# A new order of instructions and PSUM banks, and two buffers cleared on another engine, in a Conformer layer

## The chip, the cores and the metric

The kernel runs on one core of a Trainium2 chip, in one launch. The metric is the device time of that core in microseconds, the median of several runs. PE is TensorE, ACT is ScalarE, DVE is VectorE, POOL is GpSimd and SP is SyncE, which here only issues DMA transfers.

## The reference

Two sequences of 4000 tokens with 144 channels go through a Conformer layer in bfloat16. Each of its four parts normalises its input and adds its result to x; a last normalisation ends the layer:

```python
h = silu(layernorm(x) @ w_ff1a) @ w_ff1b;  x = x + 0.5 * h
q, k, v = split(layernorm(x) @ w_qkv)               # 4 heads of 36 channels
x = x + softmax(q @ k.T * 36 ** -0.5) @ v @ w_o     # over all 4000 keys
a, b = split(layernorm(x) @ w_pw1);  h = a * sigmoid(b)
x = x + silu(sum(pad(h)[i:i + T] * dw[i] for i in range(5))) @ w_pw2
h = silu(layernorm(x) @ w_ff2a) @ w_ff2b;  x = x + 0.5 * h
return layernorm(x)
```

## The kernel before

**Tiles and stages.** The 8000 tokens are 16 chunks of 500, eight to a sequence, and a chunk is four blocks of 125. For each chunk there is `pre` (first feed-forward part `ff1`, then `pre2` with queries, keys and values), then the attention of its 500 queries over all keys of its sequence (62 key tiles of 64 rows and one of 32 for all four heads), then `post1` (output projection, gated unit) and `post2` (convolution, second feed-forward part, last normalisation, store). The first sequence's `pre` makes the front; attention then runs from end to end of the kernel with the `pre` and `post` work of other chunks between; the rest of the last chunks' `post` makes the tail.

**One attention tile.** PE makes scores of four heads as four matmuls of 64x64 quads into two PSUM banks (`scores`). Then ACT takes the exp of both banks at once (`emit_exp`, 818 times), or, for 190 tiles, DVE does it with integer arithmetic in five instructions (`dve_tile`). PE multiplies the result by the values in four more quads (`o_quads`, called PV below), accumulating in banks 6 and 7. Banks 0 to 5 are shared by the scores and all other matmul results.

**Normalisations.** `ln` takes statistics on DVE, makes 1/sqrt with a pow on POOL (RS), and writes the normalised rows to a slot of XN, on POOL in the front's whole chunks and in the middle, on DVE for the first three chunks and in the tail. A slot has 640 columns, 576 of them used, and the rest must be zero because whole slots are transposed. So `ln` clears a slot at its first use, on POOL: 64 columns for a half chunk and all 640 for a whole one. `setup_dw` clears AN, the four slots for the attention's output, in one POOL instruction. A whole chunk is transposed in part by DVE (32x32 blocks), then by SP through DRAM (`blocks`: four transfers to `rows`, two back to XT or XTQ); `transp` clears the second half of an XT slot before its first use in this way, on POOL. Half chunks of the front and tail are transposed by PE instead.

**What sets the order.** The kernel is written as generators, and a planner (`Sched`, `pick_any`) with its own costs runs them and records every instruction with `Rec.op`, on which all instructions of a profile therefore have one line (L398). What is recorded between two steps of the planner on one engine is a block. `Rec.reorder` then moves the blocks of each engine by a table, ORDER: one character is the distance by which one block moves from its recorded place, its index in ALPHABET less 45; `~` begins a longer distance of two more characters. PLACES gives the PSUM bank of each of the 1724 results in recorded order. `reorder` derives the waits on PSUM banks from the order on PE and from PLACES; `finish` turns all dependences into semaphore waits, and `replay` writes one instruction stream for each engine. So ORDER and PLACES say what stands behind what on each engine, SP's DMA queue among them, and the planner's own times don't reach the chip.

Of the kernel before, what the change touches and what calls it, by code (L numbers as in the profile page):

```python
# [12 lines left out]
D = 144  # L13
# [5 lines left out]
LP = 80  # L19
FF = 576  # L20
KCONV = 5
TB = 125
# [17 lines left out]
        "PPPPPPQOQOPPPPPRPNPPQQQQLPPQORPNPRPTMORNNVO~OLNOMrMMNPMMNNNOMNNNOPLMQMMMNNPMMNSMNLMMOOPNSOMQMSPNOPU["  # L40
        "OMNRMOPPQIRMSNPNePNOOOcNNNNNNNNNOOLbNLOOQNSH]MMOLOMPMMOOOVPNOOOOPPPTOOOTPMUQMSLNNQQNQOQQNPPPPPTPPROK"
        "PPPPPPPPPPPP`PPPQKVPPKPPMPPRPUPPPROQQQRZOQQQRRKQRRSJPRRRRRRRWSZRNYUR~NHQ@R[KEGOOOPPPPKQOPPSPPSLPQMTP"
        "PPLQQQMPPPQVPPQOX_PTOPPCRTQQRGSQIQQSQRNV8OOQNNVSNOOLOPUUNN_MMWLNNRMMMMOOOPPPPPPQQNPPRSNRSSSORRVTR[OR"
        "AKQ@PPLOOQQNPPPPPUOOOOOPQOPPPPPUOOOOQRPLU`NNNXMMPNLQMNLZRNL`MN_YLLMK`KMNLILNQJMOOOPNYOPNOOOQNNZ^NNNN"
        "OOPNQNQOYP]CNNNNOMPMSO[NKOOQNVMPMMN`NbYMMMMNOMNIcLLNL[MMMNNQNRMJQLLROQSPLRNOQOPUQOMPQMPPRPVPLQOMQNPQ"
        "QQQSKPQSQKQQQQJPPPPPWQQSPKKQQUPPPSWPQRPQAVPPPQCVPQRPWHSYPHSOPQYPQEPQCPRZUPPSOOHDPR^OKOOOOPNOOOO^NOQN"
        "NOOOSNNNNS[NNNdRMNRKYNJWJNNNNNNGOOPP^YNNNNOMNNNNRNNPPPVROOLOOPPRZNNOOOOOPNOSOPNRPSMOOPQOQWNRPRLLNSZP"
        "NPQOIOQOTPPPRPQ]P^USPMMQIQKQQ8QTQQGMRRTQQKRRRRGLRSOMRPQQQJQQRPVP[OOOQEROO^IOQLNOOPPTTOMNQ[FOQNPPSPPM"
        "HPQOQQUPLOPNVPNOOSQNLUOOPNOXPPPLTQNLMPPPQOPPTOOPTPLOOQRNOPPPQOVPNOOOORZOP[PPMOOFRZOL[ROQKQTUBOKNFPPP"
        "_OOOOOOPNOOOOWNNVNNXMNTKMNOMZQOSLNOMSPSLLTPMOOUOPNOOTQOMOPPPQOPPPQOPPPTTQOSQSSSSNEEPQOPTPTMOMORSNNOP"  # L50
        "ROYPQOPQ^NPNPQOPAOOOOOSOOOPPPQQNPPPPPPXOOOOOOOaNPPPLOOOPUMOOOO[IOOPSOOQNPHPSWOOPPPPQGPPPPQQQMPPQQNPQ"
        "O_OOOPZOOOPI_NNNNZOPEOQWP^HKPHSJOLNOO`VPMRJOM^J`MPNKUNLUGNLJQNRIOPPRXOMOOOOPXMOPPMOOOPWOOPPPTKNOOPPP"
        "PPPPPPPQRPSYSQNQYZPRRRADIOXQGVOPJOORPIPPRRSSMR]MHOOQQQVRKNHPLPPPPPPPPPPRZQSQRRbHSGNQGPPQRRGLPQKQQQQJ"
        "QOQRPMQOPPQOSQNRMTROTNPXQQQEPJOQNPRPN_OPPPLRSOPLPPPGPPPSeOMPPQRJZPKLNNNN`NOKOVJNNNNcM`LMMMNNN]MNL]LL"
        "LLLLTWLXKMMVNQ_LMOPPQQ>MOOOTOMRbMMOOOOOTOOOQZIOPJMOOcOMPPT[PRORPEVHOPYCJQOQQGMOQQNQWNQNPPLSP_OaOOOPN"
        "PDPPPLOHPPQLPPPPQOTPNWNPPPWJNPPP`OIOPPPPPPPUQOELRP^TTQOZUPPCGOPQDJPPPPPPRPQWPRURPMFQQ_RPXDPQJLPNOJPN"
        "PPPPPSPPQ`PPTQQRERPQIQTNDPTPPJOPQQNPPUOPPSLPMPPRPQQRPJP[RNQQLaRJQSS[IQMGQQRPCZJPQOPQTPP@RPIPPPPQQQSS"
        "VXUQGNTQSSETDS`OQSCJQQdLOINQMRLLZMNSMMMMZLWPK]JMNLMTLNNNNVN`NNNNNROOPPJQOPLRPRMOQQRPLPXQQQRPTUQHFPQJ"
        "PPPPPPSPROUSPPTLPUOCOPNQOPROTWPRWRPVRZOY^YEOOPPMQ:;QDQQQQQQQQQEQQQMQOROVSMOTTQLVHROTRGNTVPHRPTRaJSQE"
        "QRSKNRNOQOPWQO=OOPNYOOOQNNOO]QOL_PNRO^NOUIPNK_MMW>MMMZMMMM]MMQLMMSNNOMOPPSOVNNPNXNPQOKQOQLQQQQUPPPHO"  # L60
        "QORPQMQOPQQSQOUVWNWMNOKOAOQOPPPPZWNNNOOLNNR^MNVNOMNNNNPSMN]NTNNNNNaNNNOQLN[RNOMRNHMSOSNPQGPQOPRXRPQW"
        "KOHOPPQYPPZPQRCO[I^NORFNNIZMMMNOWLNNNQMNRORRO_KPNOOOYNNNNNNOU^NSUHNKOJNOSOOQRJUPROTYMHNNURNNTMIPNQOU"
        "OOV[MNLNNNPYTNeJLNORNNGOO[]NNNNIQLMRLNRWOPUOO]OM`QO;LSOLO]JOJPRLLMRUNZMOVR[NPDOT^OOOFOSTOMNOSbPQLPRS"
        "_MORR_NPP^OHCNNNOZOWL~NHLMMNNNSOOXNOQQNSSOIVKPNPN]NOOOOOPPVOOOITNPPLPPQOWPPMRPNTKOOTNOPUMOOOQN`OOOPN"
        "OOPPPLOZOQQMPIQO^YROQQRLENO_PNPPPTQNNOROOSVO]QMNRNOPWTNOMNSOPQXbOOOQ[NO~NCdIMMMMMMMfbKMMMQMMJLMPLMUM"
        "MMNL^TR^JSLJQJUKPNLHQMPP`UNNNNOMOOOOPNOOPPPPQQNPQQQMUQQMSOPTQOPTPQUNQSPSQ<TRSSVEQQQHQQFPPPPPQSPMYTOL"
        "NNTMNNNP^[NOMNNQMMOLNN]PNOOR[OPKQN_ZLNESMOOKHOM[NPPLPNOOPPMQSTMNPQQQQRSQRRTCQVNGRNOMTTTMMNUPPQHNQSPM"
        "YVTQKLLSSOIJPSSPTMKORNOQOPPPPPPSORNSMRNRRRNQQRPFRPQQQQQQRPFQO"
    ),
    "act": (  # L70
        "PPPPPPPPPPPPPRSNNOSOOOPPPPPPPUPNOXNNOOOOOQNPPPPPPPPPROOPPQOPPPQOPPPPPPQQNPPPPPPPPPPPPPPPPPPPPPPPPPQO"
        "PPPPPPPPPPPPPPPPPPPPPPPPPPPPPPPPPPPPPPPPPPPPPPPPPPPPPPPPPPPPPPPPPPPPPPPPQOROSNOOPPPPPPPPPPPPPPPPPPPP"
        "PPPPPPPPPPPPPQOPPPPPPPPPPPPPPPPPPPPPPPPPQOPPQOPPPPPPPPPPPPPPPPPPPPPPPPPPPPPPPPPPPPPPPPPPPPPPPPPPPPPP"
        "PPPPPPPPPPPPPPPPPPPPPPPPPPPPPPPPPPPPPPPPPPPPPPPPPPPPPPPPPPPPPPPPPPPPPPPPPPPPPPPPPPPPPQOPPPPPPPPPPPPP"
        "PPPPPPPPPPPPPPPPPPPPPPPPPPPPPPQOPPQOPPPPPPPPPPPPPPPPPPPPPPPPPPPPPPPPPPPPPPPPPPPPROOPPQOPPPPPPPPPPPPP"
        "PPPPPPPPPPPPPPPPPPQOPPPPPPPPPPPPPPPPPPPPPPPPPQOQOPPPPPPPPPPPPPPPPPPPPPPPPPPPPPPPPPPPPPPPPPPPPPPPPPPP"
        "PPPPPPPPTOPNOPPPPPPPPPPPPPPPPPPPPPPPPPPPPPPPPPPPPPPPPPPPPPPPPPPPPPPPPPPQOPPPPQOPPPPPPPPPPPPPPPPPPPPP"
        "PPPPPPPPPPPPPPPPPPPPPPPPPPPPPPPPPPPPPPPROOPPQQNPPPPPPPPPPPPPPPPPPQOPPPPPPPQOPPPPPPPPPPPPPPPPPPPPPPPP"
        "PPPPPQOPPPPPPPPPPPPPPPPPROOPPPPPPPPPPPPPPPPPQOPPPPPPPPPPPPQOPPPPPPPPPPPPPPPPPPPPPPPPPPPPPPPPPPPPPPPP"
        "PQOPPPPPPPPPPPPQOPPPPPPPPPPPPPPPPPPPPPPPPPPPPPPPPPPPPPPPPPPPPPPPPPPPPPPPPPPQOPPPPPPPPPPPPPPPPPPPPPPP"  # L80
        "PPPPPPPPPPPPPPPPPPPPPPPPPPPPPPPPPQOSPNRNOQOUQNPMOPPPRORNQNPPPPPPQOROQQMPPPPPPQOPPPWORNNNOO"
    ),
    "dve": (
        "PPROQQQLPPPUUNNNNSMUNNPNOQOSPNSUMOPLOPTPNPNPPQQQQQQQQHPVPRPLPLPPPRSSNRNQVPUOODNUMPNPNPPQSPMXNOOQNNOO"
        "PPPPPPPSOOOPPQOPPPPPPPPPPPPPPPPQOQOPPPPPPROQQMQOQOPPQORSQMQQQQQRPQWQRPQLPQQQVQQQSUKTQ2KMPQQQRRORPQQR"
        "RRTQQRTTPP;RPQBPPSOOORPNSOPRPQKQOPPPPPPcPQcQQQQTPPERPDLDNRNRNQQQRFQNQQNQOPQOPPPQOPPPPPPPPPPPPPPPQQTM"
        "PPRPQQQQUQOQUQQQSQRVGPPPPSPPRPQQ/PQOPPSPPQQKPPPPPQOPPPPQOPPPPPROOPQQNROQNPPPPQOPQOQQNPPPQTQOPQRPSPRR"
        "NSPPRPQQQ;QOPPPPPPPPPPPROOQOPSOOOPQOROOUSUOOQSQHRGOPPPPROOPPQRPMQRNQNQOPPPPPPPPPPQOPRPRPQKQOPQQQRPQQ"
        "QQQWROOPQO?PPPPPPPPQOPSOPQePPROOPPEOPNOPNOOOOOQNPPPPPROOPPPPRPRRRRJQKPPQOPPPPPPPPPPPQOPPPYOOPNPRMSMR"
        "LQMPPQOPPPPPPPPPPPPPPPPPQOROOPROOPPPPPPPPQOPQOQOPPROOTOOOOQOSOOOPROQNPPPPPPPPPPPQSPPLQOPPPROOPPPPPPP"  # L90
        "PPPQOPPPPPPPPPPQOPPPPPQOPPPPPPPQQVPLTPMOLPPRPNPQOPPRRNNPROQNPPPPPPPPPPQOQOQORORNOPROOPPPQQNPPPPQOPQR"
        "NOPQOPPPPPSPNOQQNQOPQOPPPPPQQQMPPPPPPPQOPPPQOQRPMROQQMPPQOPSPNOPPUOOOOOWOOOOOOOPPQOPPQQQQRPRPQGPPPPP"
        "PPPPPPQOPPPPUOOOPNPQOSOOSNOSNZQMPLOPNOOOPPPPPPQQNQOQOPPPPQOQOPPPRUOUQOUIOJOOPPPQOPPPPUOOOOOPPPQOROQT"
        "QOPJQOPPPPPPPQQQMPQOPPQRNTNTNNNQNQOPQOROQNPPQOPPPPPPSPNOTOOOOPPPQOQQUPVQOTHPNIQOVOPPMPQMPTOPPRLTNOOO"
        "PPPPPPUOOOOOPQOPPSPSQSQSQUSTEOELQOPPPPPPPSOPNPPROOVOOPNOOPPROOVOOPNOOPQRPUQQQVRUQUPCKPDPPPPQOPPPPQOP"
        "QOQOSPNOhQOPPPPPHOPNOPPQOROQNGOOPPPQOQOPQOPRPNPPPPQOPPPPPROTPPLQRULVOUOJPNJPPQOQOPRPQMPPPPPPPPQQQQQK"
        "QRNRNORPNUOUP[LNKPMRNRNLNQSSMRMRPKQOQQNQOWPPMQOXOPRPNSOWNCPNORNRTTPJSQMSPPQRZOROQQQQTPUHOPRO4PPPPPPQ"
        "QQRLRPQLPPPPPPPPPQOQQQMPPPPPQQQMPPPPPPPPPQQQSLTRPSQJQQQQQRTOPPRPRSQSQRRTQUPQTDO/OPS]NSMOLNQQNLOVQUPU"
        "OKHPLRRNNPPPQOPQRPQQQQVQOPQORSOP?PPPPPPPPPPPPRORPQQRPWQQNPTPUPUKOO<OPQOROQQMPQOPQQNPQQSPTQNPHPPROOQS"
        "NPQULPNOORROQRPJPPSOOORO]SOSNPRWQQXPTRERGRRTTUXRTRSBSSSSSSSSAT@S&NNPPPPPPPPPPQO"  # L100
    ),
    "pool": (
        "PPPPPPRPNPPPROOPPPSOOOPPPPPQQNPQOPPPYOOOOO[NNNR`NNJOMSMMOMOXOOLNOOUORLOMROQQQRPSIOOPPSOOOPQRNOPPPTOO"
        "PNPPPPVOOPNOQNPPPRPQM"
    ),
    "sp": (
        "PPPPPPPPQOPPPPPPPPPPPPPPSOTNNOOPPPQOPPPROQNPPPPPPPPPPPPPQOPPQOQOPPPPPPPPPPPPPPQOPPPPPVOPNSNNQMPPPQOP"
        "ROYNOOOPNOOUNTNOMNPPPSOOOPPPPPPPPPPPPPQOQOPPPPQQN"
    ),
# [16 lines left out]
    "2405240524052020420442045205420524052405240524052042505240524052402505423042302420340342034203420340"  # L126
    "2342042034203420243024202430243024034202340243204303420240240334024204302430243024302340134013413412"
    "0412041201412042041204024012412140214021401241205042304231514236404512412361021452243051351241353250"
    "213024014452502542036410"
)  # L130


# [1973 lines left out]
```

## Time and profile before

| | |
|---|---|
| median of 3 runs | 881.01 us (880.66 to 881.29) |
| profiled execution, first to last instruction | 880.5 us |
| ACT, PE, DVE, POOL busy | 849.6, 851.5, 822.7, 300.4 us |
| instructions in the profile | 27000 |

A row of the page gives an engine's busy time, a group row the line, engine, operation and tiles (written <- read) with the count, then busy time and mean duration of one, then the idle time of the engine just before and what ended it. In a timeline a row begins with start and length in us, and a number in brackets is the idle time before it. In the view by stretches a row has the stretch, its length, busy time and number of instructions of PE, of PE's weight loads (PEld), of DVE, ACT and POOL, the granted TensorE clock, the busy share of the DMA engines and GB/s. A row of waits has total, times and longest.

### The profile page before, as it was taken

How to read it: one execution, taken by the hardware profiler on the slowest of the kernel's cores; microseconds unless marked ns; L12 is line 12 of the kernel's file. 1: busy time of each engine (PE TensorE's matmuls, PEld its weight loads, DVE VectorE, ACT ScalarE, POOL GpSimd, SP SyncE). 2: the span in 40 equal slices, each digit the busy share in tenths (PEclk: the TensorE clock that was granted, in tenths of full speed). 3: DMA queues.
4: the chain of work that ended last, by engine and by line, in shares of the span. 5: the costliest groups of instructions: out<-in, count | busy, mean ns of one | idle time of the engine just before them, and what ended most of it. 6: DMA issues, size and time to landing. Idle time of an engine off the chain costs nothing.

```text
span 880.5 us, 27000 instructions
## 1 busy us (share of the span) xinstructions
PE 851.5 (97%) x11419; PEld 380.2 (43%) x11419; DVE 822.7 (93%) x1812; ACT 849.6 (96%) x1098; POOL 300.4 (34%) x584
## 2 busy tenths in 40 slices
PE   8998999999999999999999999999999999999996
PEld 6543433344444443443444444344443433444366
DVE  7977999999999999999989999899999999999987
ACT  6799999999999999999999999999999999999986
POOL 7770331431336130252111813522513404032434
PEclk9999999999999999999999999999999999999999
DMA  3221001220221110212001120110110011001111
GB/s 100 44 55 38 16 18 36 62 51 16 40 49 38 23 38 22 45 24 45 16 9 30 36 44 23 23 26 20 43 31 18 21 37 20 17 12 36 27 27 33
DMA packets 114351, 28.80 MB, mean 33 GB/s; under 512 B 101090, under 2 KB 114230, under 8 KB 114230
## 3 DMA queue, kind: packets, MB, share of 16 engines
q1 hardware_dynamic: 112646, 26.39, 13.8%
q8 instruction: 89, 1.46, 0.7%
q10 hardware_dynamic: 1584, 0.69, 0.3%
q14 instruction: 32, 0.26, 0.1%
HBM read 13.44 MB, written 13.61 MB: 31 GB/s over the span
## 4 chain that ended last, share of the span: by engine, by line
ACT 46%; PE 33%; DVE 17%; POOL 2%; DMA 1%; issue 1%; SPq 1%; POOLq 0%; DVEq 0%
ACT PT L398 42%; PE PS L398 33%; DVE PT L398 7%; ACT TH L398 4%; DVE HT L398 2%; DVE ST L398 2%; DVE X L398 2%; DVE XN L398 2%; POOL RS L398 1%; POOL XN L398 1%; DVE KT L398 1%; DVE QT L398 1%; DVE AN L398 1%; SPq L398 1%; DMA rows<-XN 0%
## 5 line engine op out<-in xcount | busy, mean ns | idle before, releaser
L398 ACT ACTIVATE PT<-PS 128x1000 bf16<-128x1000 f32 (+1 forms) x818 | 757.2, 1074 | 4.1 <-PE PS L398 2.4
L398 PE MATMUL PS<-QT,KT 64*64 64x500 bf16 x3968 | 425.7, 385 | 13.0 <-ACT PT L398 5.2
L398 PE MATMUL PS<-PT,VA 64*37 64x500 bf16 x4728 | 411.5, 372 | 1.8 <-DVE QT L398 0.7
L398 DVE TENSOR_SCALAR PT<-PS 128x500 int16<-128x500 f32 x380 | 250.1, 668 | 5.8 <-PE PS L398 3.9
L398 PEld LDWEIGHTS PS<-QT,KT 64*64 64x64 bf16 x3968 | 123.4, 104 | 236.8 <-ACT PT L398 137.1
L398 POOL TENSOR_SCALAR RS<-ST 125x4 f32<-125x4 f32 x130 | 37.0, 284 | 482.2 <-DVE ST L398 475.6
L398 PEld LDWEIGHTS PS<-PT,VA 64*37 64x37 bf16 x4728 | 141.4, 96 | 96.2 <-DVE PT L398 18.7
L398 DVE TENSOR_SCALAR PT<-PT 128x1000 uint16<-128x1000 uint16 x380 | 154.5, 418 | 2.1 <-PE PS L398 0.8
L398 POOL TENSOR_SCALAR XN<-X,RS 125x144 bf16<-125x144 bf16 x260 | 150.4, 610 | 13.1 <-DMA out_dram<-XN 6.4
L398 DVE TENSOR_TENSOR PT<-PT 128x1000 bf16<-128x1000 bf16 x190 | 128.8, 679 | 1.3
L398 ACT ACTIVATE TH<-PS 128x500 bf16<-128x500 f32 (+3 forms) x194 | 107.3, 575 | 7.4 <-PE PS L398 6.5
L398 POOL TENSOR_TENSOR RS<-RS,NHALF 125x4 f32<-125x4 f32 (+1 forms) x93 | 91.7, 989 | 33.1 <-DVE RS L398 27.3
L398 DVE SCALAR_TENSOR_TENSOR HT<-TH,PS 128x500 bf16<-128x500 bf16 (+1 forms) x135 | 81.2, 615 | 12.8 <-ACT TH L398 12.0
L398 PE MATMUL PS<-XT,WA 80*128 80x500 bf16 (+5 forms) x288 | 74.5, 365 | 2.2 <-DMA XT<-rows 0.9
L398 DVE BATCH_NORM_STATS2 ST<-X 125x6 f32<-125x288 bf16 x160 | 65.7, 447 | 2.8 <-DMA X<-in_x_dram 2.7
L398 DVE SCALAR_TENSOR_TENSOR X<-PS,X 125x288 bf16<-125x288 f32 (+1 forms) x128 | 56.6, 449 | 6.5 <-PE PS L398 5.2
L398 PE MATMUL PS<-WB,HT 128*125 128x144 bf16 (+1 forms) x640 | 52.4, 230 | 0.7 <-ACT HT L398 0.5
L398 PEld LDWEIGHTS PS<-WB,HT 128*125 128x125 bf16 (+1 forms) x640 | 44.3, 136 | 14.5 <-issue 3.8
L398 PEld LDWEIGHTS PS<-XT,WA 128*128 128x128 bf16 (+1 forms) x288 | 21.2, 97 | 38.8 <-issue 10.6
L398 PE MATMUL PS<-U,DG 128*128 128x250 bf16 (+6 forms) x204 | 29.6, 264 | 0.0
L398 DVE STREAM_TRANSPOSE XN<-XN 128x320 f32<-128x320 f32 x54 | 27.0, 500 | 1.0 <-POOL XN L398 1.0
L398 POOL COPY U<-U 128x2 bf16<-128x2 bf16 (+1 forms) x54 | 9.2, 209 | 46.3 <-DVE U L398 46.3
(95 smaller groups left out, 522.6 us busy)
## 6 DMA issues: line engine op xcount, KB each, us to landing
rows<-XN SPq DMA_DIRECT2D x216, 40.0 KB, 2.0
XT<-rows SPq DMA_DIRECT2D x56, 128.0 KB, 2.0
rows<-AN SPq DMA_DIRECT2D x60, 40.0 KB, 2.0
X<-in_x_dram SPq DMA_DIRECT2D x15, 140.6 KB
XTQ<-rows SPq DMA_DIRECT2D x26, 70.3 KB
out_dram<-XN SPq DMA_DIRECT2D x13, 140.6 KB
XT<-rows SPq DMA_DIRECT2D x56, 16.0 KB, 1.9
out_dram<-XN SPq DMA_DIRECT2D x3, 70.3 KB
```

What stands on the lines that cost most here:

```text
L398: ins = getattr(eng, o.name)(*o.a, **o.k)
```

## The change

It has three parts. ORDER and PLACES are new (347 of the 1724 digits of PLACES differ, and most characters of PE's string). Nine VectorE instructions clear the five XN slots and the four AN slots whole; their blocks are recorded at the beginning and placed by ORDER. The POOL clearings of XN and AN become ghosts: the planner counts them as before, and `reorder` takes them out and hands on their dependences. And `transp` clears only three columns of each block of an XT slot (125 to 127) if the front has already written that slot whole.

```diff
 ORDER = {
     "pe": (
...
-        "PPPPPPPPPPPP`PPPQKVPPKPPMPPRPUPPPROQQQRZOQQQRRKQRRSJPRRRRRRRWSZRNYUR~NHQ@R[KEGOOOPPPPKQOPPSPPSLPQMTP"
...
+        "OQKPPPPPYOOOOYNNNOMhTNLVXLMIMOSXKILOKN`NNRRNHQOXROMQOTKOUQQQTQUS]PT[`P2ALQXDMKILMNTQLSKNRNUN_PMMNOWN"
...
     "dve": (
-        "PPROQQQLPPPUUNNNNSMUNNPNOQOSPNSUMOPLOPTPNPNPPQQQQQQQQHPVPRPLPLPPPRSSNRNQVPUOODNUMPNPNPPQSPMXNOOQNNOO"
...
+        "PROUXM~P:~P2~P<~P2KLJLLLDLNKPMILMMGSLJKLJKMJOLJTOILJHLJOQNPIFHMNNKMMMMBMXPIKINIPLLLNOCNCOQOKQQDFWUVE"
...
@@ class Rec
+        for o in self.ops:
+            drop = o.shared - o.own
+            o.deps = [(d, raw) for d, raw in o.deps if id(d) not in drop]
+        for o in self.ops:
+            if any(d.ghost for d, raw in o.deps):
+                o.deps = through(o)
+        self.ops = [o for o in self.ops if not o.ghost]
         lines = {}
...
+    def side(like, *a, **k):
+        kept = dict(R.free), R.kind, R.last, R.filling
+        R.filling = True
+        o = op(*a, cost=0.0, **k)
+        R.free, R.kind, R.last, R.filling = kept
...
+    def early(j, what, w):
+        side(None, "dve", "memset", what, 0.0, w=w).step = j / 64
+
+    for u in range(NXN):
+        early(1 + u, XNS[:, u, :], [("XN", u)])
+    for a in range(NAN):
+        early(21 + a, ANS[:, a, :], [("AN", a)])
...
     def setup_dw():
-        op("pool", "memset", ANS[:, :, :], 0.0, w=[("AN", a) for a in range(NAN)], cost=2.2)
+        op("pool", "ghost", w=[("AN", a) for a in range(NAN)], cost=2.2)
...
         if dma and s not in xt_set:
             xt_set.add(s)
-            op("pool", "memset", XT[0:LP, s, 1, :, :], 0.0, w=wk, cost=0.5)
+            whole = all((s, i) in xt_whole for i in range(NB))
+            op("pool", "memset", XT[0:LP, s, 1, :, TB:128] if whole else XT[0:LP, s, 1, :, :], 0.0, w=wk, cost=0.5)
...
+        if not inter:
+            xt_whole.update((s, i) for i in bs)
...
-            op("pool", "memset", XNS[:, u, :] if inter else XNS[:, u, n * D:n * D + 64], 0.0, w=[("XN", u)], cost=0.56)
+            op("pool", "ghost", w=[("XN", u)], cost=0.56)
...
-            op("pool", "memset", XNS[:, u, :], 0.0, w=[("XN", u)], cost=0.0)
+            op("pool", "ghost", w=[("XN", u)], cost=0.0)
```

## What was predicted

> **What bounds the kernel now.** First the page: the busy line, then the chain of waits.
>
> ```profile
> span 880.5 us, 27000 instructions
> ...
> PE 851.5 (97%) x11419; PEld 380.2 (43%) x11419; DVE 822.7 (93%) x1812; ACT 849.6 (96%) x1098; POOL 300.4 (34%) x584
> ...
> ACT 46%; PE 33%; DVE 17%; POOL 2%; DMA 1%; issue 1%; SPq 1%; POOLq 0%; DVEq 0%
> ```
>
> Three engines are nearly full, and the chain passes from one to another: ScalarE (ACT) for 46%, TensorE (PE) for 33%, VectorE (DVE) for 17%. The span is 880.5 us; the median of the three runs shown is 881.0, so 0.5 us lies outside the span, and I carry it over unchanged.
>
> Where is there room? The view of busy time by stretches, cut at the first exp on ACT, at the point where the front's work has ended, and at the last exps:
>
> ```profile
> core 0: us, PE busy (x) PEld busy (x) DVE busy (x) ACT busy (x) POOL busy (x), PEclk, DMA share, GB/s
> 0.00:19.40 19.40, 16.80 (x201) 14.48 (x201) 13.30 (x57) 11.32 (x27) 13.06 (x38) 1.00 0.43 110
> 19.40:80.00 60.60, 55.60 (x672) 25.92 (x674) 48.60 (x112) 53.00 (x79) 35.06 (x68) 1.00 0.24 51
> 80.00:840.00 760.00, 745.22 (x10162) 313.45 (x10154) 727.77 (x1533) 755.99 (x928) 235.97 (x448) 1.00 0.14 30
> 840.00:880.50 40.50, 33.85 (x398) 26.31 (x390) 33.08 (x114) 29.31 (x68) 16.35 (x31) 0.96 0.10 27
> ```
>
> Length less ACT's busy time: ACT is idle for 8.1 us before its first exp, 7.6 us in the rest of the front, 4.0 us in the 760 us of the middle, and 11.2 us in the tail. These 30.9 us are all that an order can win as long as ACT does the same work. PE is idle 5.0 us in the front and 14.8 us in the middle.
>
> **The change part by part.** The kernel first records its instructions in one order and then moves blocks of them by the strings of ORDER. I decoded both sets of strings from the diff (a character's place in ALPHABET less 45 is the shift of its block) and laid both on the same blocks. PE, ACT and SP keep exactly their instructions (11419 matmuls, 818 exps on ACT, 190 tiles of exp on DVE, 466 DMAs of SP); DVE gets nine clearings more, POOL eleven fewer. The rest is order: blocks move by 3.7 places on average on PE, 1.7 on DVE, 0.3 on ACT, 0.8 on SP. So no work is saved on the three full engines, and what can change is idle time.
>
> *The clearings.* What leaves POOL and what DVE pays, from the groups kept apart by shape:
>
> ```profile
> L398 POOL MEMSET XN<- 128x640 bf16 x5 | 3.2, 630 | 0.0
> L398 POOL MEMSET XT<- 80x512 bf16 x5 | 2.6, 519 | 0.0
> L398 POOL MEMSET AN<- 128x2560 bf16 x1 | 2.2, 2227 | 0.0
> ...
> L398 POOL MEMSET XN<- 128x64 bf16 x5 | 0.5, 145 | 0.0
> ...
> L398 POOL MEMSET U<- 80x1 bf16 x5 | 0.5, 98 | 0.3
> ...
> L398 DVE MEMSET WA<- 80x256 uint32 x1 | 0.3, 272 | 0.8 <-PEq L2091 0.8
> ...
> L398 DVE MEMSET WPZ<- 128x176 uint32 x1 | 0.2, 205 | 0.0
> ```
>
> POOL loses 3.2 + 0.5 + 2.2 = 5.9 us. Three of the five XT clearings shrink to twelve elements a row (their slot was written whole by the front); between the 98 ns row and 519 ns I take 100, the near row, so 3 x 0.42 = 1.3 us more. DVE gains nine clearings of 640 bf16, which fit into 320 words. Two rows give the slope: (272 - 205)/(256 - 176) = 0.84 ns a word, so 272 + 64 x 0.84 = 326 ns each, 2.9 us in all. Bounds: 0.27 us from below (the 256-word row), 0.63 us from above (POOL's own row for this shape).
>
> Do these 2.9 us cost anything? In the new order of DVE three XN clearings stand before the first statistics, two a few blocks on, and the four AN clearings between the copies to KT, VA and QT that run at 62 to 71 us now.
>
> ```profile
> 1.36 0.46 DVE L398 MEMSET WB<- 64x72 uint32 x3
> 3.91 0.46 DVE L398 BATCH_NORM_STATS2 ST<-X 125x6 f32<-125x288 bf16 x1 [2.09 <-DMA X<-in_x_dram]
> ...
> 67.77 0.68 DVE L398 TENSOR_SCALAR QT<-PS 128x500 bf16<-128x500 f32 x1 [2.21 <-PE PS L398]
> ...
> 71.01 1.26 DVE L398 SCALAR_TENSOR_TENSOR HT<-TH,PS 128x500 bf16<-128x500 bf16 x2 [1.98 <-ACT TH L398]
> ```
>
> The first three (1.0 us) go under the 2.09 us in which DVE waits for x; the AN clearings (1.3 us) under the gaps of 2.21 and 1.98 us. I cost them at nothing. Without that cover the first statistics would start later, 1.0 us at most, and PE and ACT would wait for the copies behind the AN clearings, 1.3 us: both stay in the range.
>
> What is POOL's relief worth? The waits for POOL:
>
> ```profile
> DVE XN L398 <- POOL RS L398: 1.3, 3, 0.7
> ...
> DVE XN L398 <- POOL XN L398: 1.0, 2, 0.7
> ```
>
> Directly DVE waits only 2.3 us for it in the whole kernel. But POOL's XN also feed the transposing transfers, and two of these are late at the end of the front:
>
> ```profile
> 69.73 1.08 PE L398 MATMUL PS<-XT,WA 128*128 128x500 bf16 x4 [0.94 <-DMA XT<-rows]
> ...
> 72.88 0.59 PE L398 MATMUL PS<-XTQ,WK 72*128 72x500 bf16 x2 [0.90 <-DMA XTQ<-rows]
> ```
>
> Both sit on the chain. In POOL's new order the fourth whole-chunk normalisation stands before the three short RS operations it followed until now, and the clearings between are gone, so the later XN come some us earlier. I let both waits vanish: **-1.8 us**, with 0 and -4.1 (the 2.3 us of DVE as well) as ends. What is late next there is SP, which issues these transfers one after the other.
>
> *The front's order.* ACT's largest gap after the first exp, and PE at that time:
>
> ```profile
> 32.19 1.82 ACT L398 ACTIVATE TH<-PS 128x500 bf16<-128x500 f32 x4 [3.34 <-PE PS L398]
> 33.87 1.04 ACT L398 ACTIVATE PT<-PS 128x1000 bf16<-128x1000 f32 x1
> ```
>
> ```profile
> 28.91 2.80 PE L398 MATMUL PS<-WB,HT 128*125 128x144 bf16 x40
> 31.54 1.52 PE L398 MATMUL PS<-XT,WA 128*128 128x500 bf16 x6
> ```
>
> ACT waits 3.34 us while PE runs four residual blocks of ten matmuls (40 from 28.91 to 31.54 us, so 0.66 us a block) ahead of the next FF tiles. The new order puts three FF tiles ahead of the last of these blocks: ACT's TH come 0.66 us sooner. It also puts two exps right ahead of those TH, the one of 33.87 us and one that ran before the gap. That could fill more, but DVE is nearly full at that time, so I take **-0.6 us**, with +1 (if the residual, now later, is what DVE waits for) and -2.6 as ends.
>
> *The middle.* What a change between kinds of matmul costs on PE:
>
> ```profile
> 48.39 0.41 PE L398 MATMUL PS<-QT,KT 64*64 64x500 bf16 x4
> 48.62 0.80 PE L398 MATMUL PS<-PT,VA 64*37 64x500 bf16 x12
> 49.26 0.38 PE L398 MATMUL PS<-QT,KT 64*64 64x500 bf16 x4
> 49.57 0.60 PE L398 MATMUL PS<-XTQ,WK 72*128 72x500 bf16 x2
> 50.09 0.41 PE L398 MATMUL PS<-QT,KT 64*64 64x500 bf16 x4
> ```
>
> Twelve PV matmuls take 0.64 us from start to start, 0.053 each, so four take 0.21; the four scores before WK take 0.31 and WK's two take 0.52 for some 0.42: the step from quads to whole-array matmuls and back costs 0.10 us each way. The old order has 797 changes of kind, the new one 792: -0.5 us. Steps between scores and PV fall from 1434 to 1399, but cost at most 0.02 us (0.23 for the four scores of 48.39), so nothing. [...]
>
> Then the distances. From the last score matmul of an ACT exp to the first PV matmul on its result PE has 40 matmuls at the median in the old order and 52 in the new, 22 and 26 at the tenth percentile. A PV that comes later waits less:
>
> ```profile
> PEld PS L398 <- ACT PT L398: 148.3, 406, 1.1
> PEld PS L398 <- issue: 81.6, 263, 0.5
> PEld PS L398 <- DVE PT L398: 68.9, 223, 0.8
> ```
>
> Most of this lies under running matmuls, and ACT has 4.0 us left in the middle, so I take -0.5 us for it: with the switches **-1.0 us**, ends -4 (all of ACT's idle time there) and +7 (the last rival).
>
> *The tail.* About every block moves and the banks differ, but instructions and their dependences are the same; nothing in the trace says which way it goes:
>
> ```profile
> 875.66 0.69 POOL L398 TENSOR_TENSOR RS<-RS,NHALF 125x2 f32<-125x2 f32 x1 [0.32 <-DVE RS L398]
> ```
>
> I take **0**, with ends of -1.5 and +1.5: two such RS operations of POOL, on which a last normalisation waits, more or fewer on the final path.
>
> Sum: -1.8 - 0.6 - 1.0 = -3.4 us; 880.5 - 3.4 = 877.1 us of span, and 0.5 more outside: **877.6 us**.
>
> **The rivals.** *More comes back.* With PV later and POOL free, ACT could lose 4 of its 7.6 us in the front, 2 of 4.0 in the middle and 1.5 in the tail: -7.5, 873.5 us. For it: all engines' orders were moved at once, and POOL, which feeds the normalisations, goes without a gap worth a row from 12 to 31 us:
>
> ```profile
> 12.27 4.40 POOL L398 TENSOR_TENSOR RS<-RS,NHALF 125x2 f32<-125x2 f32 x6 [4.36 <-DVE RS L398]
> ...
> 32.85 1.39 POOL L398 TENSOR_TENSOR RS<-RS,NHALF 125x2 f32<-125x2 f32 x2 [2.06 <-DVE RS L398]
> ```
>
> Against it: POOL then waits 2.06 us for DVE, which is the next limit.
>
> *Given back.* The late transfers stay late. The rows that speak for it:
>
> ```profile
> q8 instruction: 89, 1.46, 0.7%
> ...
> rows<-XN SPq DMA_DIRECT2D x216, 40.0 KB, 2.0
> ```
>
> Each of the 89 instruction packets takes 0.7% x 16 x 880.5 / 89 = 1.1 us of one DMA engine, about half the 2.0 us of a landing. If the two transfers of the front's end each meet one, 2.2 us come back of the 1.8 + 0.6 won there, and with the middle unchanged the time is 880.8 us. [...] That the change doesn't do what it says (clearings that were hidden on POOL anyway, one order as good as the other) gives the same: 881.0.
>
> *Slower: the banks turn over too fast.* Between the last matmul into a PSUM bank and the first score matmul that reuses it PE has 18 matmuls at the lower quartile in the old order and 16 in the new, 12 and 10 at the fifth percentile. Where ACT sets the pace this costs nothing. Where PE does (33% of the chain, so 265 of the 802 score pairs), two matmuls less are 2 x 0.053 = 0.105 us of waiting for each pair whose exp isn't back. If that is the lowest quarter of them, 66 pairs, it is 7 us against the 2.4 of the front and the 0.5 of the switches: 881.0 + 7.0 - 2.9 = 885.1 us. It decides from 28 such pairs on (28 x 0.105 = 2.9 us). For it: PE already waits for exps 406 times. Against it: the median hardly moves (22 to 21), and half banks for DVE tiles keep their 14 and 18.
>
> **How the numbers follow.** Forecast 0.47, more comes back 0.14, given back 0.13, slower 0.26. A measurement of this kernel tells about 0.2%, 1.8 us, from no change. Faster by more than that is 0.47 + 0.14 = 0.61, within it 0.13, slower 0.26. The likeliest case alone reaches from 875.0 (POOL's far end) to 879.2. For 8 in 10 the range reaches from the larger gain to just past the slower case: 873.0 to 886.0, which leaves out some 0.05 below and 0.12 above.
>
> **What would show it.** Right: the waits of PE for XT and XTQ at 68 to 73 us are gone; ACT's 3.34 us gap near 29 us is under 2.8; DVE's nine clearings last 0.33 us each and its other work isn't later; ACT's idle time from 19.4 to 80 us falls from 7.6 to near 5 and stays under 4 in the middle. Wrong: ACT's idle time in the middle grows with PE waiting for banks (the slower rival), or the front is shorter and the middle takes it back. A tail over 42 us after the last exps would upset the sum as well, since I gave it nothing.

## The result, and the profile after

The changed kernel takes 883.76 us (median of 6 runs, 883.49 to 884.29) against 880.94 us for the kernel before (6 runs, 880.47 to 881.29): a ratio of 1.0032, 95% interval 1.0020 to 1.0043. It is slower by 2.8 us, where 3.4 us less were forecast. Its profiled execution took 883.61 us, with a span of 881.8.

First the page of the changed kernel, its busy line and its chain:

```profile
span 881.8 us, 27051 instructions
...
PE 846.5 (96%) x11419; PEld 385.9 (44%) x11419; DVE 824.2 (93%) x1821; ACT 850.1 (96%) x1098; POOL 293.8 (33%) x573
...
ACT 50%; PE 29%; DVE 14%; POOL 4%; issue 1%; DMA 1%; SPq 0%; POOLq 0%; DVEq 0%
```

ACT's work is the same, POOL has 6.6 us less and DVE 1.5 us more. Now the view by stretches of the changed kernel, cut at the same points as before:

```profile
core 0: us, PE busy (x) PEld busy (x) DVE busy (x) ACT busy (x) POOL busy (x), PEclk, DMA share, GB/s
0.00:19.40 19.40, 16.60 (x202) 14.36 (x203) 15.43 (x62) 11.33 (x27) 12.22 (x33) 1.00 0.44 111
19.40:80.00 60.60, 57.88 (x690) 26.95 (x688) 51.74 (x119) 55.55 (x80) 29.63 (x62) 1.00 0.23 51
80.00:840.00 760.00, 740.77 (x10187) 320.09 (x10190) 726.43 (x1537) 756.54 (x930) 234.27 (x445) 1.00 0.14 29
840.00:881.80 41.80, 31.26 (x356) 24.48 (x345) 30.60 (x106) 26.66 (x64) 17.72 (x35) 0.95 0.11 30
```

Length less ACT's busy time: ACT is idle for 5.05 us in the front (7.6 before), 3.46 in the middle (4.0) and 15.1 in the tail (11.2). So the front and the middle did what was forecast, and at 840 us all three full engines are ahead: ACT has 26.7 us of work left instead of 29.3, PE 31.3 instead of 33.9, DVE 30.6 instead of 33.1. Yet the span ends 1.3 us later. The loss is in the last 40 us.

Two rows end the stretches of the tail, the last exps on ACT and the last normalised rows on DVE (timelines of the changed kernel):

```profile
838.59 3.27 ACT L419 ACTIVATE PT<-PS 128x1000 bf16<-128x1000 f32 x4
```

```profile
875.26 0.54 DVE L419 TENSOR_SCALAR XN<-X,ST,RS 125x144 bf16<-125x144 bf16 x2 [0.36 <-POOL RS L419]
```

The exps end at 841.87 us, the last XN at 875.80, and the span at 881.8. I call what lies between them **the closing work** (last exp to last XN of DVE: 33.9 us here) and **the landing** (last XN of DVE to the end: 6.0 us here). In the profile before they are 32.06 and 3.59 us. Every comparison below is made in these pieces, since the first, the time of the last exp, differs by 1.5 us among executions of one and the same order up to there (844.87 us before, 843.33 in p1 below). In the profiles of four experiments (e3, o1, p2, p4) the granted clock was 0.84 to 0.91 in stretches of the first 80 us, so that their rows are read only from the last exp on.

### The profile page after: what moved, and what is told of

It reads as the page before. It is cut to its first block, busy times and chain, and to the rows that moved or that the text cites. A ratio compares the mean times of both kernels' runs of the same rounds, so it can differ in the third digit from the quotient of the medians.

```text
span 881.8 us, 27051 instructions
## 1 busy us (share of the span) xinstructions
PE 846.5 (96%) x11419; PEld 385.9 (44%) x11419; DVE 824.2 (93%) x1821; ACT 850.1 (96%) x1098; POOL 293.8 (33%) x573
## 3 DMA queue, kind: packets, MB, share of 16 engines
q8 instruction: 90, 1.47, 0.7%
## 4 chain that ended last, share of the span: by engine, by line
ACT 50%; PE 29%; DVE 14%; POOL 4%; issue 1%; DMA 1%; SPq 0%; POOLq 0%; DVEq 0%
ACT PT L419 46%; PE PS L419 29%; DVE PT L419 6%; ACT TH L419 4%; POOL XN L419 2%; POOL RS L419 2%; DVE HT L419 2%; DVE ST L419 2%; DVE XN L419 1%; DVE X L419 1%; DVE QT L419 0%; DMA XT<-rows 0%; DVE KT L419 0%; SPq L419 0%; DVE AN L419 0%
## 5 line engine op out<-in xcount | busy, mean ns | idle before, releaser
L419 PE MATMUL PS<-QT,KT 64*64 64x500 bf16 x3968 | 419.6, 384 | 15.5 <-ACT PT L419 8.2
L419 PE MATMUL PS<-PT,VA 64*37 64x500 bf16 x4728 | 403.6, 372 | 1.0 <-DVE QT L419 0.5
L419 POOL TENSOR_SCALAR RS<-ST 125x4 f32<-125x4 f32 x130 | 39.9, 307 | 462.6 <-DVE ST L419 456.2
L419 DVE TENSOR_SCALAR PT<-PT 128x1000 uint16<-128x1000 uint16 x380 | 152.1, 415 | 2.1 <-PE PS L419 1.0
L419 POOL TENSOR_SCALAR XN<-X,RS 125x144 bf16<-125x144 bf16 x260 | 147.1, 595 | 8.3
L419 ACT ACTIVATE TH<-PS 128x500 bf16<-128x500 f32 (+3 forms) x194 | 101.7, 542 | 5.8 <-PE PS L419 5.1
L419 POOL TENSOR_TENSOR RS<-RS,NHALF 125x4 f32<-125x4 f32 (+2 forms) x93 | 91.8, 990 | 32.1 <-DVE RS L419 26.7
L419 PE MATMUL PS<-XT,WA 80*128 80x500 bf16 (+4 forms) x288 | 75.2, 364 | 4.8 <-DMA XT<-rows 1.6
L419 PE MATMUL PS<-U,DG 128*128 128x250 bf16 (+7 forms) x204 | 28.7, 265 | 0.1
```

The source lines that it names most:

```text
L419: ins = getattr(eng, o.name)(*o.a, **o.k)
```

## The experiments

They ran on other chips than the first result, so each is read as a ratio to the kernel before on its own chip (881.5 to 882.0 us there). The changed kernel itself ran only on the chip of the first result. A block is the unit that ORDER moves. Where an edit changes whole strings, the fence tells it in words.

**e1: the six stores at the end.** SP issues its last six stores in the old sequence again, the one of 144 KB (o15) ahead of two that wait for ACT. One string differs:

```diff
 "sp": (
-"...PPPPRXNNOOOOORNOPQORPN"
+"...PPPPRXNNOOOOORNOPPPPQO"
```

> The changed kernel with only SP's last six stores in the order of the kernel before: the two whole-chunk stores o12 and o15 go ahead of the small ones that wait for the last normalisations. Theory S (the new order loses its gain because the last stores are issued together and the end waits for them): o15 can leave at about 873.3 us instead of 874.9, so that the last store lands about 1.2 us earlier; time 882.5, between 881.8 and 883.0. Theory M (the end waits for the last instructions, whichever store goes first): within 0.3 us of 883.8.

Measured: 883.25 us, 1.0018 (1.0009 to 1.0027). The landing falls from 6.0 to 5.5 us, the closing work stays at 33.95. A part of the loss, but not most of it; the interval overlaps that of the changed kernel.

**e2 and e3: a store moved behind the transposing transfer.** In the changed kernel a store (o10) stands on SP between the four last transfers to `rows` and the two to XT. e2 moves it behind them, e3 does both edits.

```diff
 "sp": (
-"...PPPPRXNNOOOOORNOPQORPN"
+"...PPPPRZNNOOOOOQNNPQORPN"
```

> The changed kernel with only one store, o10, moved on SP's queue from between the two steps of a transposing transfer to behind it. Theory S: the store is what makes XT<-rows land 3.7 us after its issue where 2.0 is usual; PE's wait of 1.2 us for it at 850 us goes, and the tail is 1.0 us shorter, time 882.7. Theory M: the landing is late for another reason, time within 0.3 us of 883.8.

> Both edits on SP's queue in the changed kernel. Theory S: the two gains add up to about 2.2 us, time 881.5. Theory M: within 0.4 us of 883.8.

Measured: 887.69 us, 1.0064 (1.0052 to 1.0077), and 886.12 us, 1.0056 (1.0043 to 1.0068). Both are misses, and worse than the change: the closing work grows to 36.9 and 38.1 us. The timeline of ACT in e2 shows why:

```profile
851.61 0.90 ACT L419 ACTIVATE XN<-X,RS 125x144 bf16<-125x144 bf16 x2 [2.71 <-DMA out_dram<-XN]
```

ACT's next normalisation writes the XN slot that the store o10 reads, and waits until that store has landed. In the changed kernel the wait is 1.01 us (SP issues o10 at 845.95 us, its last landing update comes at 849.61, ACT starts at 849.69); issued later, the store makes it 2.71. (After the stall the granted clock of e2 is also lower, 0.88 and 0.78 from 850 to 860 us.)

**e4: the kernel before with the new sequence of the six stores.**

```diff
 "sp": (
-"...QOPPPPQQN"
+"...QOPPPPQQNPPPQORPN"
```

> The kernel before with only SP's last six stores in the new kernel's order. Theory S: o15 leaves about 4 us later, together with the last small ones, and the end comes 1 to 1.5 us later: 882.0 to 882.5. Theory M: within 0.3 us of 880.9.

Measured: 887.24 us, 1.0061 (1.0047 to 1.0075), far more than expected. The same mechanism: DVE waits 3.5 us for a slot that a late store still holds, and ACT then 5.0 us for DVE's RS. The landing, too, grows from 3.6 to 5.7 us. So here the sequence of the stores has to fit the order of the engines that reuse the slots.

**h1 and h2: the tail exchanged.** h1 is the changed kernel with the old order and banks for all that is recorded from the end of attention on, h2 the reverse.

```diff
 ORDER and PLACES of h1, blocks and results recorded
   up to the end of attention: as in the changed kernel
-  from there on: as in the changed kernel
+  from there on: as in the kernel before
```

> The changed kernel with the order and the banks of the kernel before for everything recorded from the end of the attention on (the tail); front, middle and clearings as changed. Theory T (front and middle won about 3 us, since the switch to the Silu table comes at 842.7 us instead of 845.9, and the tail of the new order loses 4.5): the old tail of 34.7 us starts 3 us earlier, time 877.5 to 878.5. Rival B (the new tail is long because of the state that the new middle leaves, such as late chunks, held XN slots and stores): the old tail's order meets the same late chunks, time 881 to 884.

> The kernel before with the order and the banks of the changed kernel for the tail alone. Theory T: 4.5 us more from the table switch to the end and about 1 us more outside the span, time 885 to 887. Rival B: the tail's order is not what loses, time within 1 us of before.

Measured: h2 884.78 us, 1.0034 (1.0022 to 1.0046): the new tail alone costs all that the change costs, though less than theory T said. h1 882.42 us, 1.0008 (0.9999 to 1.0016): with the old tail most of the loss goes, but ACT's lead doesn't become time, as rival B had it. The timeline of SP in h1 gives a reason, which lies in where I split the order:

```profile
846.09 0.27 SPq L419 DMA_DIRECT2D out_dram<-XN  x1
846.40 0.59 SPq L419 DMA_DIRECT2D X<-X  x1
847.04 2.60 SPq L419 DMA_DIRECT2D rows<-XN  x4
```

The store o10 and a halo transfer now stand ahead of the last transfers to `rows`, whose XN POOL had written by 842.3 us and DVE had transposed by 844.6.

**c1 and o1: the clearings alone, the order alone.** c1 is the changed code with ORDER and PLACES of before (the nine clearings keep their places), o1 the new order with the clearings on POOL.

```diff
 c1: ORDER, PLACES
-  as in the changed kernel
+  as in the kernel before
 o1: clearings of XN and AN
-  DVE, early
+  POOL, as before
```

> The order and the banks of the kernel before, with only the clearings of XN and AN on DVE (in the changed kernel's places) and the shorter XT clearings. The prediction's step (POOL's relief makes the two late transfers at the end of the front come in time): -1.8 us, 879.1. Rival (POOL's clearings lay under waits, and in the old order nothing is late for them): within 0.5 us of before.

> The new order and banks with all clearings on POOL as before (put behind the block that precedes them in the old order). If the front's gain is the order's: within 0.7 us of the changed kernel, 883.5 to 884.5. If it is the clearings': the front loses its 2.5 us, 885.5 to 886.5.

Measured: c1 882.14 us, 1.0002 (0.9994 to 1.0011): POOL's relief alone is worth nothing. o1 884.97 us, 1.0038 (1.0026 to 1.0051): the order alone costs what the change costs.

**n1 and n2: one normalisation back in its place.** Comparing where each block of POOL stands in both orders shows one that is far off: the last normalisation of a whole chunk. The kernel before runs it in the middle, the changed one in the tail (timelines of POOL, before and after):

```profile
792.74 0.20 POOL L398 TENSOR_SCALAR RS<-ST 125x4 f32<-125x4 f32 x1
793.02 1.04 POOL L398 TENSOR_TENSOR RS<-RS,NHALF 125x4 f32<-125x4 f32 x1
794.13 1.05 POOL L398 TENSOR_SCALAR RS<-ST 125x4 f32<-125x4 f32 x1
795.28 3.55 POOL L398 TENSOR_SCALAR XN<-X,RS 125x144 bf16<-125x144 bf16 x4
```

```profile
842.41 0.20 POOL L419 TENSOR_SCALAR RS<-ST 125x4 f32<-125x4 f32 x1
842.68 1.04 POOL L419 TENSOR_TENSOR RS<-RS,NHALF 125x4 f32<-125x4 f32 x1
843.79 0.23 POOL L419 TENSOR_SCALAR RS<-ST 125x4 f32<-125x4 f32 x1
844.13 1.79 POOL L419 TENSOR_SCALAR XN<-X,RS 125x144 bf16<-125x144 bf16 x4
```

What it feeds is the store o10. The timeline of SP in the changed kernel has that store right ahead of the two transfers to XT:

```profile
842.43 2.55 SPq L419 DMA_DIRECT2D rows<-XN  x4
845.95 0.28 SPq L419 DMA_DIRECT2D out_dram<-XN  x1
846.40 0.82 SPq L419 DMA_DIRECT2D XT<-rows  x2
```

The chain of the changed kernel then has one of these transfers, the one of 16 KB, at 3.71 us, where the page gives 1.9 as the median, and the timelines of PE and ACT show who waits:

```profile
846.78 3.71 DMA XT<-rows
```

```profile
850.54 0.63 PE L419 MATMUL PS<-XT,WA 128*128 128x500 bf16 x2 [1.19 <-DMA XT<-rows]
```

```profile
849.69 0.90 ACT L419 ACTIVATE XN<-X,RS 125x144 bf16<-125x144 bf16 x2 [1.01 <-DMA out_dram<-XN]
```

n1 moves the three blocks of this normalisation (statistics on DVE, RS and XN on POOL, the store on SP) back to where the kernel before has them; n2 adds e1's edit.

```diff
 changed kernel, order of blocks
-DVE  ...statistics of the chunk later, POOL ...RS, XN at 842 us, SP ...rows, o10, XT
+DVE  ...statistics, POOL ...RS, XN behind the normalisation of o9, SP ...o9, o10, XT ... rows, XT
```

> The changed kernel with one normalisation moved back to its old place: the last normalisation of one whole chunk (two statistics blocks on DVE, RS and four XN on POOL, store o10 on SP). The kernel before runs it on POOL at 792.7 to 798.8 us, the changed one at 842.4 to 845.9 us, in the tail. Nothing else is changed. Theory N (this normalisation is what spoils the new tail: its store of 141 KB runs beside the last transposing transfer and holds an XN slot that ACT waits for, its statistics take 0.7 us of DVE, which has no gap there): PE's waits for XT in the tail fall from 4.1 to under 2 us, ACT's wait for the store goes, and the ratio to the kernel before falls from 1.0032 to 1.0010-1.0020, so 1 to 2 us. Rival (the tail is bound by its own order of blocks and by the six stores at the end, and this normalisation lies beside it): 1.0028 to 1.0036.

> As n1_ln_back, and SP's last six stores in the order of e1_stores_spread. Theory N, if the two costs add: 1.0000 to 1.0010, since the order of the stores alone gave 1.4 thousandths. Rival: 1.0014 to 1.0022, as e1 alone. If it is no faster than n1, the two are one cost: whichever is late holds the end.

Measured: n1 882.91 us, 1.0018 (1.0009 to 1.0027), the closing work down from 33.9 to 32.7 us, and no wait for XT or a slot is left in the tail. So by the profiles this is 1.3 us of the loss, and the landing is still 6.0. n2 882.72 us, 1.0018 (1.0007 to 1.0029): the two edits don't add up. Its landing is 5.7 us.

**h5 and h3: the old tail without the fault of that split, and the front alone.** h5 is h1 with the same normalisation moved back; in h3 only what is recorded up to about 80 us has the new order.

```diff
 h5 = h1, and the normalisation of o10 with its store moved back
 h3: ORDER, PLACES from about 80 us on
-  as in the changed kernel
+  as in the kernel before
```

> As h1_before_tail (the new front and middle, the old order and banks from the end of attention on), with the same normalisation and its store moved back. In h1 the store o10 and the halo transfer stood on SP ahead of the last four transfers to rows, which went out at 847.0 instead of 842.4 us. Theory N: the last XT is there some 3 to 4 us earlier, PE doesn't wait for it, and the lead of ACT (2 to 3 us at the end of attention) becomes time: ratio 0.9970 to 0.9990, 879.0 to 880.8 us beside a before of 881.7. Rival (DVE's 24 us without a gap at the end set the tail, and a lead of ACT never was one of DVE): 1.0003 to 1.0012, as h1.

> The new order and banks up to about 80 us (the front, with the clearings on DVE), the old ones from there to the end. It tells whether the 2.5 us that ACT wins in the front are still there at the end. Theory (a lead of the front runs through, since the middle in its old order has almost no slack that could take it): ratio 0.9968 to 0.9980, 2 to 2.8 us. Rival (the middle gives it back: DVE, at 93%, and the transposing transfers are not ahead, and ACT waits for them later): 0.9995 to 1.0008, with ACT's idle time from 80 to 840 us up from 4.0 to over 5.5.

Measured: h5 880.86 us, 0.9991 (0.9983 to 1.0000), 1.5 us less than h1 in the ratio and just short of the range expected; the best of all kernels here, though its interval reaches 1. h3 881.65 us, 1.0001 (0.9992 to 1.0010): a miss. In h3's profile the closing work is 32.05 us, to a hundredth that of the kernel before, but the landing is 4.67 instead of 3.59. The views of the DMA queues from 874 to 882 us show what is different, here for h3:

```profile
DMA packets 392, 0.22 MB, mean 28 GB/s; under 512 B 16, under 2 KB 391, under 8 KB 391
## 3 DMA queue, kind: packets, MB, share of 16 engines
q10 hardware_dynamic: 258, 0.14, 6.9%
q1 hardware_dynamic: 133, 0.07, 3.2%
q14 instruction: 1, 0.01, 0.2%
```

One instruction packet (8 KB, at 877.56 us) falls among the stores. In the record of its packets 576-byte rows follow that packet one at a time until 879.05 us, while the others have ended by 878.1. The record names no engine; I take these rows for those of one DMA engine. The kernel before has no such packet after 854 us.

**p1 to p4: that packet.** It is there in each kernel whose DVE stream has 1856 to 1858 records in the profile, not where it has 1845 to 1852; with 1854 (c1) it comes at 881.46 us, after the last store. So the clearings' number could have a price. p1 adds twelve small clearings of an unused buffer on DVE to the kernel before; p2, p3 and p4 make the nine clearings of the changed kernel, of h5 and of h3 in three instructions.

```diff
 p1, kernel before
+    SCR = sb("SCR", [384])
...
     def zero_e(eng, WE, nm):
+        for j in range(12 if eng == "dve" else 0):
+            op(eng, "memset", SCR[0:LP, 32 * j:32 * j + 32], 0.0, cost=0.0)
         op(eng, "memset", WE[0:LP, 1, 64:128], 0.0, w=[(nm, "z", 1)], cost=0.1)
 p2 to p4
-    for u in range(NXN):
-        early(1 + u, XNS[:, u, :], [("XN", u)])
-    for a in range(NAN):
-        early(21 + a, ANS[:, a, :], [("AN", a)])
+    early(1, XNS[:, :, :], [("XN", u) for u in range(NXN)])
+    for a in range(0, NAN, 2):
+        early(21 + a, ANS[:, a:a + 2, :], [("AN", a), ("AN", a + 1)])
```

> The kernel before with twelve more clearings of 32 columns of an unused buffer on DVE at the very start (some 1 us there, under DVE's wait for x), nothing else. DVE's stream in the profile has then 1857 records instead of 1845. In every kernel so far whose DVE stream has 1856 to 1858 records, an 8 KB instruction packet falls at 875 to 878 us among the last stores (changed kernel 876.46, front only 877.56); with 1845 to 1849 there is none, with 1854 (clearings alone) it comes at 881.5, after the end. Theory P (DVE's longer stream brings that packet, and one DMA engine is late with the last store because of it): the packet appears at 874 to 878 us, the last store lands about 4 us after its issue instead of 3.0, and the ratio is 1.0006 to 1.0014. Rival (the packet belongs to another engine, or costs nothing): no packet there, or one with 3.0 us to landing, ratio 0.9995 to 1.0005.

> The changed kernel with its nine clearings on DVE made in three instructions (all of XN in one, AN in two pairs) at the place of the first of each, so six instructions fewer on DVE: 1852 records. Theory P: the packet of 876.46 us goes behind the end, the last store lands some 5.2 us after its issue as in the old order with the new tail, not 5.5 to 6, and the ratio falls from 1.0032 to 1.0020-1.0026. Rival: unchanged, 1.0030 to 1.0036, or worse if the longer clearings hold up the copies behind them.

> The new front and middle, the old tail, one normalisation back (h5_before_tail_ln_back), with the clearings in three instructions: 1851 records on DVE. There the packet fell at 875.16 us and the last compute instruction ended 1.5 us earlier than with clearings alone, but the span only 1.1. Theory P: 0.3 to 0.8 us less than h5, ratio 0.9982 to 0.9988. Rival: 0.9991 as h5.

> The new front alone (h3_front_only) with the clearings in three instructions: 1850 records. In h3 the last XN of DVE ended 1.24 us earlier than with clearings alone, and the last store took 4.1 us from issue to landing instead of 3.1, with the packet at 877.56 us in between, so that nothing of the lead was left. Theory P: the last store lands in 3.0 us again and the ratio falls from 1.0001 to 0.9986-0.9992. Rival (the landing is late for another reason, or the lead is only noise of one profile): 0.9997 to 1.0005.

Measured: in p1 the packet appears, at 875.02 us, and in p2, p3 and p4 it is gone: their views have no row of q14 from 874 us on (to 880 us in p2, to the end in p3, to 882 in p4). The landing follows it each time: p1 4.03 us against 3.59 before; p4 3.58 against 4.67 in h3; p3 3.58 against 4.11 in h5; p2 5.20 against 6.00 in the changed kernel. SP's waits for the stores, h3 and p4:

```profile
SPq L425 <- DMA out_dram<-XN: 3.6, 3, 1.6
```

```profile
SPq L425 <- DMA out_dram<-XN: 2.5, 3, 1.0
```

In time the effect is not settled. p2 takes 883.30 us, 1.0019 (1.0010 to 1.0029), where the changed kernel has 1.0032 (1.0020 to 1.0043), and the two intervals overlap. p1 is 881.86 us, 1.0003 (0.9994 to 1.0011), p3 881.25, 0.9995 (0.9987 to 1.0004), p4 881.27, 0.9999 (0.9987 to 1.0011): three misses. The packet's 0.4 to 1.1 us in the profiles are about as large as the intervals, and p3 gave 0.35 us back in its closing work (33.06 against 32.71). That the landing is longer with the packet is shown in four pairs of profiles, by 0.4 to 1.1 us; what it costs in the median is not.

**q1 and q2: the two stores priced.** q1 is the changed kernel writing one row of the store o15 instead of 125, q2 one row of o10.

```diff
             q = f"o{len(outs)}"
+            if q == "o15":
+                dst, src = dst[0:1], src[0:1]
```

> The changed kernel, with the store o15 reduced from 125 rows to one: 143 of the 144 KB of output that it writes are left out, all else (its wait, its place behind o18 and o16 on SP) stays. It prices the six stores that are issued together at the end. Theory S2 (they share some 100 KB/us, by 54 KB in half a microsecond at the best, so the last lands when all 428 KB are through): 1.4 us less to the last landing, 4.1 us after the last issue instead of 5.5, ratio 1.0014 to 1.0020. Rival (the late landing is the instruction packet's and the number of stores', not the bytes'): 5.0 to 5.5 us, ratio 1.0026 to 1.0034.

> The changed kernel, with the store o10 reduced from 125 rows to one (140 KB of output left out), at its place in the tail between the transfers to rows and the two to XT; its normalisation stays where it is. n1_ln_back, which moves normalisation and store back, took 1.3 us off the stretch from the last exp to the last XN of DVE (33.9 to 32.7). This tells the store's part from the normalisation's. Theory D (the store beside the XT transfer and the XN slot that it holds): PE's wait for XT in the tail and ACT's wait for the slot fall, the stretch is 32.6 to 33.1 us, ratio 1.0018 to 1.0024. Rival (DVE's statistics and POOL's 4 us are what counts): 33.6 to 34.0 us, ratio 1.0028 to 1.0036.

Measured: q1 882.71 us, 1.0013 (1.0004 to 1.0022); the landing is 4.67 us instead of 6.00, and the last store lands 4.2 us after its issue, as the theory of the bytes had it. The rows of the DMA view from 874 to 882 us, changed kernel and q1:

```profile
DMA packets 651, 0.44 MB, mean 55 GB/s; under 512 B 25, under 2 KB 650, under 8 KB 650
```

```profile
DMA packets 523, 0.30 MB, mean 37 GB/s; under 512 B 21, under 2 KB 522, under 8 KB 522
```

q2 882.64 us, 1.0011 (1.0003 to 1.0020), a little less than the range expected; the closing work is 32.70 us, to 0.03 us that of n1, though the normalisation is still in the tail. PE's and ACT's instructions that had waited go on without a gap (timelines of q2):

```profile
849.12 0.61 PE L419 MATMUL PS<-XT,WA 128*128 128x500 bf16 x2
```

```profile
848.58 0.91 ACT L419 ACTIVATE XN<-X,RS 125x144 bf16<-125x144 bf16 x2
```

So it is the store, not the normalisation's arithmetic on DVE and POOL. Whether it costs by its bytes beside the transfer to XT or by the slot that it holds was not separated.

## Why the prediction was wrong

The pieces side by side, each from one profiled execution:

| kernel | last exp ends | closing work | landing |
|---|---|---|---|
| before | 844.87 | 32.06 | 3.59 |
| p1 (before, twelve clearings more) | 843.33 | 32.04 | 4.03 |
| h3 (new front) | 843.40 | 32.05 | 4.67 |
| h5 (new front and middle) | 842.42 | 32.71 | 4.11 |
| h2 (new tail) | 844.16 | 33.76 | 5.16 |
| after | 841.87 | 33.94 | 6.00 |

**The base: 0.5 us outside the span was wrong, and the profiled execution wasn't a typical one.** In all runs that show both numbers the time is 1.8 to 2.1 us above the span, 1.8 in most. The median of 881.0 us thus belongs to a span of 879.2, and the execution with 880.5 was 1.3 us slower than the median. Part of what I counted as winnable was that execution's own: the rows of the same wait of PE in c1 and in p1, both with the old order,

```profile
70.06 1.08 PE L419 MATMUL PS<-XT,WA 128*128 128x500 bf16 x4 [1.18 <-DMA XT<-rows]
```

```profile
68.94 1.09 PE L398 MATMUL PS<-XT,WA 128*128 128x500 bf16 x4 [0.34 <-DMA XT<-rows]
```

and the wait for XTQ behind it, 0.90 us in the profile I read, isn't there in either. Taken together the two were 1.84 us there, 1.18 in c1, 0.34 in p1, and in e4 and h2, which have the old front too, 1.47 and 0.60.

**The clearings on DVE: right in size, hidden as forecast, and not quite free.** The rows by shape of the changed kernel:

```profile
L419 DVE MEMSET XN<- 128x320 uint32 x5 | 1.6, 325 | 0.2
L419 DVE MEMSET AN<- 128x320 uint32 x4 | 1.3, 325 | 0.1
```

325 ns against 326, and the front is no later for them. What I hadn't thought of is that an instruction packet comes to lie among the last stores (at 876.46 us here; h5 has one there too, and p3, which is h5 with the clearings in three instructions, has none from 874 us to its end).

**POOL's relief, -1.8: failed as a cause.** The two waits did vanish, but with the clearings alone they don't (c1's row above), and c1's time is that of before. It takes the new order (of which engine was not tried), and what goes is the part that is there in a given execution. Nor did both waits sit on the chain, though I wrote so: from 61 to 73 us it runs through SP, a transfer to `rows` and the one to XTQ, and PE's wait for XT isn't on it.

**The front's order, -0.6: the gain is there, and larger, but it comes from the part that I counted as nothing.** The gap of 3.34 us on ACT, the same in all five profiles with the old front (before, c1, e4, h2, p1), is now

```profile
28.87 1.90 ACT L419 ACTIVATE PT<-PS 128x1000 bf16<-128x1000 f32 x2 [0.76 <-PE PS L419]
31.92 1.54 ACT L419 ACTIVATE TH<-PS 128x500 bf16<-128x500 f32 x3 [1.15 <-PE PS L419]
```

```profile
28.75 2.09 PE L419 MATMUL PS<-WB,HT 128*125 128x144 bf16 x30
31.26 1.54 PE L419 MATMUL PS<-XT,WA 128*128 128x500 bf16 x6 [0.42 <-DMA XT<-rows]
```

One residual block less stands ahead of the FF tiles, as forecast, but PE then waits 0.42 us for XT, and ACT's TH come 0.27 us sooner (31.92 against 32.19) instead of 0.66. The two exps ahead of them fill the gap. With both terms ACT wins 2.5 us in the front against the profile I read (2.4 forecast), and 1.3 against p1's. ACT is idle in the front for 6.35 to 7.60 us in the five profiles with the old front and for 4.92 to 5.54 in the eleven with the new one and a granted clock of 1.00 there, so the gain is no accident of one execution.

**The middle, -1.0: right in direction, about half as large.** ACT's idle time there falls by 0.6 us (4.0 to 3.46), and from h3 to h5, which differ in the middle and in what stands at the tail's start, by 0.5 (4.33 to 3.82). The last exp comes 1.0 us earlier in h5 and the time falls by 0.8 us, but a part of that lies ahead of 80 us, where both have one order, and their intervals overlap. PE's weight loads do wait less for exps, as forecast (148.3 and 68.9 us before):

```profile
PEld PS L419 <- ACT PT L419: 144.5, 404, 0.9
PEld PS L419 <- DVE PT L419: 58.7, 185, 0.8
```

What the fewer changes of kind give was not tried by itself. The rival of the PSUM banks came near the time (885.1) but not by its mechanism. The rows of the scores, before and after:

```profile
L398 PE MATMUL PS<-QT,KT 64*64 64x500 bf16 x3968 | 425.7, 385 | 13.0 <-ACT PT L398 5.2
```

```profile
L419 PE MATMUL PS<-QT,KT 64*64 64x500 bf16 x3968 | 419.6, 384 | 15.5 <-ACT PT L419 8.2
```

PE does wait 3 us more for exps to free their banks, but ACT, which sets the pace there, waits less, so it costs nothing.

**The tail, 0 with ends of 1.5: this is the step that failed.** "Instructions and their dependences are the same; nothing in the trace says which way it goes" was true of the trace and not of the change: I had decoded the new strings, and they say that the store o10 moves from the middle into the tail, and that SP's six last stores come in another sequence. I averaged these moves ("0.8 on SP") instead of looking at the ones that go far. I also took for granted that a lead of ACT at the end of attention becomes time. Measured against the median of before (last exp at 881.0 - 1.8 - 35.65 = 843.55 us): the lead is 1.7 us, half of the 3.4 forecast, the closing work costs 1.9 and the landing 2.4, so +2.6 where the medians say +2.8. Of the 1.9, the store o10 is 1.2 (q2) and the rest the new order of the tail (n1 still has 32.7 against 32.06). Of the 2.4, the packet is 0.8 (p2) and the six stores that go out together at the end (three by SP, three by ACT; before, two and two) 1.6 (h2 and p2, whose views show no packet of 8 KB: 5.2). The warning that I set at 42 us after the last exps was too wide: they were 39.9 us, against 35.7 before, and that was enough.

The closing work divides at one instruction, PE's matmul on the last XT. What follows it takes 22.8 us in the profiles with the old tail (before, c1, p1, h1, h3, h5, p3) and 25.3 to 25.4 in those with the new one (after, h2, n1, q2). It starts 9.3 us after the last exp in the kernel before, in c1, p1 and h3, and 7.3 us in n1 and q2, where XT is in time. So the new order comes to this matmul 2 us sooner, has 2.5 us more behind it, and loses whatever XT is late: 1.19 us in the changed kernel, beside the store o10, and 0.67 in h2. h2 has no o10 in its tail; its last transfers to `rows` go out 2.2 us after the last exp, 0.6 in the changed kernel. The timelines of PE, before and h2:

```profile
854.14 1.95 PE L398 MATMUL PS<-XT,WA 128*128 128x500 bf16 x12
```

```profile
852.66 0.63 PE L398 MATMUL PS<-XT,WA 128*128 128x500 bf16 x2 [0.67 <-DMA XT<-rows]
```

One smaller slip: the far end of POOL's relief gives 877.6 - 2.3 = 875.3 us, not the 875.0 from which I took the likeliest case.

"Given back" had an instruction packet in the way of a transfer, and so it came, but at the last store and not at XT. Its 2.2 us, a packet's whole 1.1 us for each of two transfers, were my estimate. One case near it stands in the profile before: the last transfer to `rows` ahead of XTQ lands 3.6 us after its issue at 65.33 us and the two to XT beside it after 3.2 and 3.0, where the page's medians are 1.9 to 2.0, and an instruction packet of 16 KB runs from 66.75 to 67.90 us. In the changed kernel no such packet falls into that time, and the two to XT land after 2.2 and 1.8 us. In the tail the packet took 0.31 us in the changed kernel and about 0.7 in p1, and the landing grew by 0.4 to 1.1 us in the four pairs; in the changed kernel (0.8) the packet's length alone gives too little.

What stays open: why the old tail behind the new middle needs 0.65 us more closing work in h5 and 1.0 in p3 (the rows show a part: the last exp comes 0.98 us earlier in h5 than in h3, the last transfers to `rows` only 0.28, and PE waits 0.40 us for XT in p3), and why n2's two edits don't add up in time though its pieces are shorter. The new order and the new banks were never tried one without the other. That the best kernel here, h5, beats the kernel before is not settled; its interval ends at 1.0000.

## What to carry to other kernels

When an order is changed as a whole, look for the few blocks that move far and ask what each brings with it (a store, the buffer that it holds until it lands, its place in a DMA queue), instead of judging by the mean shift. A lead in the engine that bounds the middle is not time saved until it has been followed through the stage after it, down to the landing of the last store. And before a wait is counted as a gain, see whether it is as long in another execution of the same kernel.

## What the runs showed of the hardware

- **The last stores keep five to six of the 16 DMA engines busy.** Five stores of 124 or 125 rows and one of a single row leave 25 packets under 512 bytes (the fence of the changed kernel under q1), of 4 bytes each, and as many landing updates (besides one that each store has 0.4 to 0.6 us after its issue): 5 for each store of 125 rows, 4 for the one of 124, 1 for the single row. With o15 reduced to a row the packets are 21. I read that as a store of 125 rows running in five parts; in the same trace each of the four last transfers to `rows` has 16 such updates. Several stores together were no wider: from 876 to 879 us the busy share of the 16 engines is 0.36, 0.34 and 0.33 in the changed kernel, and without the instruction packet the packets' time adds up to 5.3 to 5.5 engines. A 576-byte row took 29 ns (median of 500), so five at a time would give some 99 KB/us; the view by stretches shows 89 to 107 GB/s in these three us. The last 430 KB took from 875.0 to 880.7 us. A store cut into smaller ones was not tried.
- **Here a store kept its source buffer until it landed** (changed kernel: ACT writes o10's slot 0.08 us after the last landing update), so a store issued later can cost more than one that runs beside an urgent transfer (e2: 2.71 us of waiting instead of 1.01).
